# Fused linear attention and GELU MLP: w_in tiles 8 and 9 of chunk 0 side by side, k of batch 0 from a second queue, batch 1's kv and x by halves

## The chip, the cores and the metric

One core of a Trainium2 chip. The metric is the device time of one execution in microseconds (us); each kernel is timed several times, the median is quoted, and the runs of the other kernel are taken in the same rounds on the same chip. A profile's times count from its first instruction ("the span", about 1.8 us shorter than the device time here).

## The reference, cut to what matters

```python
# q, k, v: (8 batches, 8 heads, 576, 64) f32
q_s = softmax(q, over head_dim);  k_s = softmax(k, over seq)
kv  = einsum("bhsd,bhse->bhde", k_s, v)
x   = einsum("bhsd,bhde->bhse", q_s, kv)      # -> (4608 tokens, 512)
h   = x @ w_in                                # 512 x 2048
out = gelu(h) @ w_out                         # exact gelu (erf); 2048 x 512
```

## The kernel before

Nine chunks of 512 tokens: one per batch, and one of the batches' rests. A chunk's w_in stage (64 matmuls of 128x512, a gelu per tile of 4) is followed by its w_out stage (64 matmuls). Attention of a later batch is woven into these. The argument is about chunk 0, where the loads still arrive, and the passage to chunk 1:

```python
touch = singles.tile([16, 4, 2], FP32)        # tiny first reads of k, v, w_in, w_out, from ScalarE
for i, a in enumerate((k[0]..., v[0]..., moe_w_in[...], moe_w_out[...])):
    nc.scalar.dma_start(out=touch[:, i, :], in_=a)
load_main(0, "q", q, 2)                       # two halves, from SyncE
load_pair(0, "k", k, 2)
load_pair(0, "v", v, 4)
wi = [load_wi(i) for i in range(5)]
...
h_phase(0, {...casts of w_in and w_out...}, groups={0: 2, 4: 4}, ybanks=(6, 8))
...
for t in range(12): y_part(t, range(J))       # chunk 0's w_out stage, 4 matmuls a step
tp_step(1, 0); tp_step(1, 1)                  # transposes of batch 1's q
y_part(12, range(J)); y_part(13, range(J))
kv_step(1)                                    # 72 small matmuls, then VectorE's norm
y_part(14, range(J)); y_part(15, (0, 1))
y_out(0, yps[0], 0); y_out(0, yps[1], 1)      # VectorE
x_mm(1, 0); x_mm(1, 1)                        # batch 1's x, then its copies
y_part(15, (2, 3))
h_phase(1, ...)                               # chunk 1's w_in stage
```

`groups={0: 2, 4: 4}` says which tiles of w_in's stage run side by side (step by step over the contraction); `ybanks` says which tiles use a bank of the idle w_out pool in PSUM, the memory that matmuls write to.

The softmax here doesn't subtract the row's maximum and nothing guards it: scores larger than these inputs give would overflow.

## Time and profile before

| | before |
|---|---|
| time, median (first three runs) | 280.57 us (280.5 to 281.31) |
| TensorE busy in the profile | 98% of 278.9 us |
| q's second half of batch 0 landed | 5.78 us |
| v's last piece of batch 0 landed | 12.38 us |
| chunk 0, first w_in matmul | 14.57 us |
| chunk 0, first w_out matmul | 29.16 us |
| chunk 1, first w_in matmul | 45.44 us |
| chunk 2, first w_in matmul | 75.39 us |

The starts up to chunk 1 are those of TensorE's timeline, chunk 2's is that of its piece in the chain that ended last; their differences are taken as the length of each stage. From chunk 2 on all kernels here run alike, so the start of chunk 2 tells a kernel's lead or lag. The profile's lines are shown in the prediction.

### The profile page before, as it was taken

What the parts mean: (1) busy time and instruction counts of PE and PEld (TensorE: products, weight loads), DVE (VectorE), ACT (ScalarE), POOL (GpSimd) and SP (SyncE); (2) the same over time, 40 slices, a digit from 0 to 9 for tenths busy, and PEclk for the clock granted to TensorE, in tenths of its full rate; (3) what the DMA queues carried; (4) which work ended last, traced back from release to release, by engine and by line L of the source; (5) the groups of instructions that cost most, each with busy time, mean ns of one, the idle gap of its engine ahead of it and who ended that gap; (6) DMA issues with size and microseconds to landing.
All of it is one profiled execution on the core that took longest, in us unless ns stands there. A gap on an engine that the chain in (4) does not pass through costs nothing.

```text
span 278.9 us, 4564 instructions
## 1 busy us (share of the span) xinstructions
PE 272.2 (98%) x1922; PEld 125.8 (45%) x1922; DVE 102.1 (37%) x152; ACT 157.0 (56%) x243; POOL 33.0 (12%) x25
## 2 busy tenths in 40 slices
PE   7899999999999999999999999999999999999995
PEld 3343454444444444444444444444444444444443
DVE  3767486309753530093007500651015200130012
ACT  5747665689377816691569346943683263036400
POOL 1530050002020130004000500050005000000000
PEclk9999999999999999999999999999999999999999
DMA  7999999962993139812981189117501500120033
GB/s 237 385 405 428 399 401 407 399 257 74 305 352 64 41 109 240 329 38 73 256 349 41 40 219 384 49 66 185 119 0 75 150 2 0 75 78 0 0 78 76
DMA packets 44996, 50.10 MB, mean 180 GB/s; under 512 B 20400, under 2 KB 29872, under 8 KB 44720
## 3 DMA queue, kind: packets, MB, share of 16 engines
q1 hardware_dynamic: 44688, 49.68, 53.3%
q8 instruction: 15, 0.25, 0.3%
q10 hardware_dynamic: 288, 0.13, 0.2%
q14 instruction: 5, 0.04, 0.1%
HBM read 36.70 MB, written 9.44 MB: 165 GB/s over the span
## 4 chain that ended last, share of the span: by engine, by line
PE 91%; DMA 7%; DVE 1%; ACTq 0%; issue 0%
PE ps L308 44%; PE ps L298 42%; DMA w<-in_moe_w_in_dram 3%; DMA f<-in_v_dram 2%; PE kv L166 2%; DMA touch<-in_moe_w_in_dram 2%; PE ps L254 1%; PE ps L330 1%; DVE wi_bf L381 0%; ACTq L433 0%; PE ps L259 0%; PE ps L215 0%; PE tp L215 0%; DVE y_sb L335 0%; PE xx L254 0%
## 5 line engine op out<-in xcount | busy, mean ns | idle before, releaser
L298 PE MATMUL ps<-xT,wi_bf 128*128 128x512 bf16 x576 | 126.4, 379 | 0.3
L308 PE MATMUL ps<-wo_bf,g 128*128 128x512 bf16 x560 | 124.2, 379 | 0.0
L303 ACT ACTIVATE g<-ps 128x512 bf16<-128x512 f32 x144 | 85.2, 597 | 69.3 <-PE ps L298 69.3
L298 PEld LDWEIGHTS <-wi_bf 128*128 128x128 bf16 x576 | 56.2, 98 | 68.9 <-DVE wi_bf L381 1.0
L308 PEld LDWEIGHTS <-g 128*128 128x128 bf16 x560 | 53.9, 98 | 64.6 <-issue 0.8
L315 DVE COPY y_sb<-ps 128x512 f32<-128x512 f32 x35 | 23.9, 686 | 81.4 <-PE ps L308 81.1
L198 POOL TENSOR_TENSOR e<-e,recq 128x2048 bf16<-128x2048 bf16 (+1 forms) x9 | 25.7, 2856 | 178.1 <-DVE recq L197 150.0
L145 DVE CAST v_aug<-f 128x576 bf16<-128x576 f32 x26 | 17.9, 745 | 46.9 <-DMA f<-in_v_dram 46.9
L196 DVE TENSOR_REDUCE qsum<-e 128x16 f32<-128x1024 bf16 (+1 forms) x13 | 21.0, 1615 | 13.9 <-ACT e L133 13.9
L280 ACT CAST xT<-ps 128x512 bf16<-128x512 f32 x19 | 10.3, 589 | 26.7 <-PE ps L254 17.1
L133 ACT ACTIVATE e<-f 128x512 bf16<-128x512 f32 (+1 forms) x42 | 20.5, 556 | 2.4 <-DMA f<-in_q_dram 2.0
L138 ACT ACTIVATE ek<-f 128x2304 bf16<-128x2304 f32 (+1 forms) x10 | 17.2, 1730 | 1.8 <-DMA f<-in_k_dram 1.8
L278 DVE CAST xT<-ps 128x512 bf16<-128x512 f32 x15 | 9.7, 687 | 17.5 <-PE ps L254 14.6
L79 ACT ACT_TABLE_LOAD x9 | 11.5, 1283 | 2.8 <-issue 2.6
L415 PE MATMUL ps<-zeros 128*128 128x512 f32 (+1 forms) x14 | 8.6, 764 | 1.5 <-DVE zeros L447 1.5
L133 ACT ACT_TABLE_LOAD x7 | 9.0, 1283 | 0.1
L381 DVE CAST wi_bf<-w 128x512 bf16<-128x512 f32 x12 | 7.4, 661 | 2.6 <-DMA w<-in_moe_w_in_dram 2.3
L166 PEld LDWEIGHTS <-ek 64*64 64x64 bf16 x576 | 6.3, 105 | 2.6 <-issue 1.1
L166 PE MATMUL kv<-v_aug,ek 64*64 64x65 bf16 x576 | 6.9, 193 | 0.0
L198 DVE TENSOR_TENSOR e<-e,recq 128x1024 bf16<-128x1024 bf16 x4 | 6.4, 1606 | 0.1
L254 PE MATMUL ps<-qT,kvc 64*64 64x512 bf16 x60 | 5.0, 390 | 1.0 <-DVE kvc L177 1.0
L408 DVE CAST wo_bf<-w 128x2048 bf16<-128x2048 f32 (+1 forms) x4 | 4.4, 1090 | 3.9 <-DMA w<-in_moe_w_out_dram 3.9
(35 smaller groups left out, 42.8 us busy)
## 6 DMA issues: line engine op xcount, KB each, us to landing
out_dram<-y_sb SPq DMA_DIRECT2D x32, 256.0 KB, 2.3
f<-in_k_dram SPq DMA_DIRECT2D x6, 1152.0 KB, 10.0
f<-in_v_dram SPq DMA_DIRECT2D x6, 1152.0 KB, 11.7
f<-in_q_dram SPq DMA_DIRECT2D x6, 1024.0 KB, 7.1
w<-in_moe_w_in_dram SPq DMA_DIRECT2D x6, 512.0 KB, 8.9
f<-in_k_dram SPq DMA_DIRECT2D x4, 576.0 KB, 10.0
f<-in_v_dram SPq DMA_DIRECT2D x8, 288.0 KB, 7.8
f<-in_q_dram SPq DMA_DIRECT2D x4, 512.0 KB, 8.5
```

The costliest lines, as they stand in the source:

```text
L79: nc.scalar.activation(out=scr[:, 1:2], in_=scr[:, 0:1], func=func)
L133: nc.scalar.activation(out=dst[:, i], in_=src[:, u], func=AF.Exp)
L138: nc.scalar.activation(out=ek[b % 2][:, i:i + n], in_=st[b]["kf"][:, i:i + n].rearrange("p x (n d) -> p x n d", n=NS), func=AF.Exp,)
L145: eng.tensor_copy(out=v_aug[b % 2][:, hp, :, 0:D], in_=st[b]["vf"][:, hp, :].rearrange("p (n d) -> p n d", n=NS),)
L166: nc.tensor.matmul(ps[c, i, half, 0:D + 1], ek[b % 2][pr, hp, n, :], v_aug[b % 2][pr, hp, n, 0:D + 1], start=(n == 0), stop=(n == NS - 1),)
L196: nc.vector.reduce_sum(out=qsum, in_=eq[:, :, hs, :], axis=AX.X)
L198: eng.tensor_tensor(out=eq[:, :, hs, :], in0=eq[:, :, hs, :], in1=recq.unsqueeze(3).to_broadcast([128, J, w, D]), op=ALU.mult,)
L280: nc.scalar.copy(out=st[b]["xT"][:, hp, :], in_=ps)
L298: nc.tensor.matmul(ps, wi_bf[:, dm, t * 128:(t + 1) * 128], xT[:, dm, :], start=(dm == 0), stop=(dm == NDM - 1),)
L303: nc.scalar.activation(out=g[:, t, :], in_=ps, func=AF.Gelu)
L308: nc.tensor.matmul(ps, st[c]["g"][:, t, j * 128:(j + 1) * 128], wo_bf[:, t, :], start=(t == 0), stop=(t == NDF - 1),)
L315: nc.vector.tensor_copy(out=y_sb, in_=ps)
```

## The change

Its intent: read k first and with real data instead of a touch; let each cast of w_in feed two matmuls; load batch 1's last v pair between the last two rows of w_out; cut batch 1's kv and x in halves so that TensorE can work on w_out while these arrive.

```diff
# load_pair: the first piece of k of batch 0 from ScalarE's queue
+            h0 = i * n
+            if b == 0 and name == "k" and i == 0:
+                nc.scalar.dma_start(out=f[:, 0, :], in_=src[:, 0, :])
+                h0 = 1
+            nc.sync.dma_start(out=f[:, h0:(i + 1) * n, :], in_=src[:, h0:(i + 1) * n, :])
# q and k are now issued ahead of the touches; the touch of k is gone (cut)
-    load_pair(1, "v", v, 4)
-    load_wo_end(wo[3])
+    for hp in range(3):
+        load_v1(hp)
+    load_wo_row(wo[3], 2)
+    load_v1(3)
+    load_wo_row(wo[3], 3)
-    }, groups={0: 2, 4: 4}, ybanks=(6, 8))
+    }, groups={0: 2, 4: 4, 8: 2}, ybanks=(6, 8))
-    for hp in range(3):
+    for hp in range(HP):
         cast_v(1, hp, nc.gpsimd)
# the passage into chunk 1 (cut: the x_tile and xx lines, cast_v(1, 3), the place of the last cast_wo)
-    kv_step(1)
+    kv_mm(1, 0)
+    kv_norm(1, 0, 1)
     y_part(14, range(J))
-    y_part(15, (0, 1)) ... y_out of 0 and 1 (cut)
+    x_mm(1, 0)
+    kv_mm(1, 1)
+    x_evac(1, 0, "s"); x_evac(1, 1, "s")
+    kv_norm(1, 1, 2)
+    y_part(15, range(J))
+    y_out(0, yps[0], 0)
+    y_out(0, yps[1], 1, "s")
     x_mm(1, 1)
     x_evac(1, 2)
-    x_evac(1, 3)
-    y_part(15, (2, 3))
+    x_evac(1, 3, "s")
```

More of the change, by code (lines that the diff above doesn't have):

```diff
@@ L97, in load_pair, with load_v1 @@
         for i in range(parts):
-            nc.sync.dma_start(out=f[:, i * n:(i + 1) * n, :], in_=src[:, i * n:(i + 1) * n, :])
+            h0 = i * n
[3 more added lines that the diff above has]
+            nc.sync.dma_start(out=f[:, h0:(i + 1) * n, :], in_=src[:, h0:(i + 1) * n, :])
+    def load_v1(i):
+        if i == 0:
+            st[1]["vf"] = f32in.tile([128, HP, NS * D], FP32, tag="vf", name="f")
+        src = v[1].rearrange("h (p n) d -> (h p) (n d)", n=NS)
+        nc.sync.dma_start(out=st[1]["vf"][:, i, :], in_=src[i * 128:(i + 1) * 128, :])
     def load(b):
@@ L311, in y_mm, with y_out @@
         )
-    def y_out(c, ps, j):
+    def y_out(c, ps, j, eng="v"):
         y_sb = moe_sb.tile([128, DM], FP32, tag="y_sb")
-        nc.vector.tensor_copy(out=y_sb, in_=ps)
+        if eng == "v":
+            nc.vector.tensor_copy(out=y_sb, in_=ps)
+        else:
+            nc.scalar.copy(out=y_sb, in_=ps)
         if c < B:
@@ L398, in load_wo, with load_wo_row @@
         return w
-    def load_wo_end(w):
+    def load_wo_row(w, c):
         src = moe_w_out[3 * 512:4 * 512, :].rearrange("(p c) f -> p c f", c=4)
-        for c in (2, 3):
-            nc.sync.dma_start(out=w[:, c], in_=src[:, c])
+        nc.sync.dma_start(out=w[:, c], in_=src[:, c])
     def cast_wo(i, w, c0=0, n=4, eng="v"):
@@ L425, in warm_x @@
                 )
-    touch = singles.tile([16, 4, 2], FP32)
-    for i, a in enumerate((k[0].rearrange("h (p n) d -> (h p) (n d)", n=NS)[0:128:8, 0:2],
-                           v[0].rearrange("h (p n) d -> (h p) (n d)", n=NS)[0:128:8, 0:2],
+    load_main(0, "q", q, 2)
+    load_pair(0, "k", k, 2)
+    touch = singles.tile([16, 3, 2], FP32)
+    for i, a in enumerate((v[0].rearrange("h (p n) d -> (h p) (n d)", n=NS)[0:128:8, 0:2],
                            moe_w_in[0:128:8, 0:2], moe_w_out[0:512:32, 0:2])):
         nc.scalar.dma_start(out=touch[:, i, :], in_=a)
-    load_main(0, "q", q, 2)
-    load_pair(0, "k", k, 2)
     load_pair(0, "v", v, 4)
@@ L511 @@
     tp_step(1, 1)
-    cast_v(1, 3)
     load(3)
     cast_wo(3, wo[3], 2, 1, "s")
+    cast_wo(3, wo[3], 3, 1, "s")
     y_part(12, range(J))
     y_part(13, range(J))
-    kv_step(1)
-    cast_wo(3, wo[3], 3, 1, "s")
+    kv_mm(1, 0)
+    kv_norm(1, 0, 1)
     y_part(14, range(J))
-    y_part(15, (0, 1))
-    y_out(0, yps[0], 0)
-    y_out(0, yps[1], 1)
     x_tile(1, 0, psum_a, "a")
     x_tile(1, 1, psum_h, "h")
+    x_mm(1, 0)
+    kv_mm(1, 1)
+    x_evac(1, 0, "s")
+    x_evac(1, 1, "s")
+    kv_norm(1, 1, 2)
+    y_part(15, range(J))
+    y_out(0, yps[0], 0)
+    y_out(0, yps[1], 1, "s")
     xx = psum_a.tile([128, 2, M], FP32, tag="a2", name="xx")
     st[1]["x2"], st[1]["x3"] = xx[:, 0], xx[:, 1]
-    x_mm(1, 0)
     x_mm(1, 1)
-    x_evac(1, 0, "s")
-    x_evac(1, 1, "s")
     x_evac(1, 2)
-    x_evac(1, 3)
-    y_part(15, (2, 3))
+    x_evac(1, 3, "s")
     y_out(0, yps[2], 2)
```

## The prediction

> **What bounds the kernel now.** I read the page first (busy shares, slices), then the chain that ended last, then who waited for whom on TensorE in the first 30 us, then single instructions of chunk 0, because the first two views say that only the front can move. The page's busy line and the clock line of its slices:
>
> ```profile
> PE 272.2 (98%) x1922; PEld 125.8 (45%) x1922; DVE 102.1 (37%) x152; ACT 157.0 (56%) x243; POOL 33.0 (12%) x25
> ...
> PEclk9999999999999999999999999999999999999999
> ```
>
> TensorE is busy 98% of 278.9 us at full clock; no other engine passes 56%. The chain that ended last, in order of time (start, us, what):
>
> ```profile
> 5.97 6.41 DMA f<-in_v_dram
> 12.38 0.02 issue
> 12.40 9.27 DMA w<-in_moe_w_in_dram
> 21.67 0.02 issue
> 21.69 1.16 DVE wi_bf L381 x2
> 22.85 0.05 issue
> 22.89 6.43 PE ps L298 x29
> 29.33 10.36 PE ps L308 x48
> ...
> 45.51 13.96 PE ps L298 x64
> ...
> 75.39 13.81 PE ps L298 x64
> ```
>
> The reader is to see two regimes. Up to 22.9 us loads set the end: batch 0's v, then w_in, then two VectorE casts of w_in. From there on the chain is TensorE alone, without a hole to the last output. A full chunk's 64 matmuls of w_in take 13.81 us, 0.2158 us each, and nothing in this change touches that. So all there is to win is (a) the time before chunk 0's first w_in matmul, (b) holes inside chunk 0's w_in stage and (c) holes between chunk 0's w_out stage and chunk 1.
>
> (b) TensorE's timeline has these lines (start, us, ..., count, idle before):
>
> ```profile
> 14.23 0.41 PE L254 MATMUL ps<-qT,kvc 64*64 64x512 bf16 x4 [0.60 <-DVE kvc L177]
> 14.57 14.75 PE L298 MATMUL ps<-xT,wi_bf 128*128 128x512 bf16 x64
> 29.16 10.52 PE L308 MATMUL ps<-wo_bf,g 128*128 128x512 bf16 x48
> ```
>
> From 14.57 to 29.16 are 14.59 us for 64 matmuls that need 13.81: 0.78 us of holes. The waits of the weight loads between 14 and 29 us name most of them (total, times, longest):
>
> ```profile
> PEld L298 <- DVE wi_bf L381: 1.0, 2, 0.6
> ```
>
> The single matmul starts place them: 18.47 to 18.89 (0.20 us over the pitch, released by a gelu that frees a PSUM tile), 21.91 to 22.37 (0.25 over) and 22.37 to 22.90 (0.31 over). The last two, 0.56 us, are tile 8's third and fourth contraction steps waiting for the casts of w_in's fourth block: its first half landed at 20.43, its second at 21.67, and each cast takes 0.62 us.
>
> (c) From 29.33 to 45.51 the chain has 16.18 us; 64 w_out matmuls (13.81), 16 transposes (0.90), 72 kv (0.71) and 8 x (0.56) make 15.98. Holes and mode changes are worth 0.2 us.
>
> **What the Trainium skill says.** "TensorE: Matmul & The Clock Gate", section "Back-to-back issue gap", has N/2.4 + 2.5 ns for a single-matmul gap, 216 ns at N=512; the trace's 215.8 ns agrees, though the page also gives 131 ns as the sustained value, which this trace contradicts. "DMA: Bandwidth & Descriptors", section "Issuing engines are not separate DMA queues": transfers of Scalar and Sync run on the same 16 DMA engines and interleave. The trace agrees in that DMA is near full (0.9 or more) in the slices from 7 to 56 us while nearly all is issued by one engine; a second issuer finds no spare bandwidth. "PSUM — Partial Sum Buffer", section "PSUM bank collisions raise a hardware error": two engines may not access one bank at once, reads included. The kernel before has both copies of the two-bank tile xx on VectorE, so its trace cannot show it; in the new order ScalarE's copy of the second half does wait for VectorE's of the first.
>
> **The change, part by part.**
>
> *1. k of batch 0 first, part of it from ScalarE, its touch gone.* Same bytes, one 0.3 MB piece of k (128 x 2304 B = 0.295 MB) now queued at 0.74 us beside q instead of a tiny touch. q's halves (0.524 MB) landed at 4.41 and 5.78, so the rate is 0.383 MB/us and the piece costs 0.77 us. Whichever way the two queues interleave, q's second half lands after it: later by 0.45 (if the cold ramp before 3 us overlaps) to 0.77. That half feeds exp, row sum, normalisation (VectorE, ends 10.35), transposes at 10.49, first kv half at 11.46. From there by durations, without the waits for v: first kv norm 11.99, x 12.54, second kv half 12.78, its norm, x 13.82, first w_in matmul 14.17, against a measured 14.57 that v's last piece (landed 12.38, GpSimd cast to 13.11) sets. So the q path has 0.40 us of slack, and the start slips by 0.05 to 0.37 us. The v path may come up to 0.3 us earlier, since k's first reads (5 to 6 us, 300 GB/s against 383) now overlap q; that gains nothing as long as q decides.
>
> *2. Tiles 8 and 9 side by side.* No instruction added. Each cast step now feeds two matmuls (0.43 us) against 0.62 us of a cast, with a head start: counting from 21.69, step three is due at 22.55 (cast done near 22.31) and step four at 22.98 (cast done 22.85). The 0.56 us of holes close. Tile 9 needs a PSUM tile that gelu 4 frees at 21.83; it is due at 21.91, so at most a hole of some 0.02 us. With a slipped start there is even more room. w_in stage ends at 28.58 + slip against 29.16: gain 0.56 - slip, 0.2 to 0.5.
>
> *3. v's last pair between rows 2 and 3, cast on GpSimd.* Before, v's pieces landed at 39.20, 39.89, 40.61, 41.36, the rows at 41.99 and 42.62. Swapped, row 2 lands near 41.3 and pair 3 near 42.0; GpSimd casts (0.67 us) to 42.7. The second kv half is due near 43.8 less the gain, so it is hidden. Row 2 is cast (0.62, ScalarE) by 41.9, due at 42.6 less the gain; row 3 by 43.25, due at 44.2 less the gain. All hold for gains up to 0.6; the old order would have waited for row 2 (cast by 42.64, due at 42.95 less the gain) for gains over 0.3. So this part protects part 2 rather than gains.
>
> *4. kv and x by halves, copies moved.* Same matmuls, two more switches between 128-row and 64-row work, about 0.1 us each by the starts around 44.3 (44.04 to 44.35 is 0.31 against a 0.22 pitch). It removes the 0.06 hole and some waits in sequence, and PE alone reaches chunk 1 at 45.49 against 45.44. New ends: y_out of tile 0 follows the second kv norm on VectorE (44.33 to 44.85, then 0.69) and frees chunk 1's first PSUM tile at 45.5, some 0.05 late; x's last copy on ScalarE follows VectorE's (46.3 + 0.6 = 46.95) where the fourth step is due at 46.83, 0.15 late with the wait's latency. Net cost of 4: about 0.2 us.
>
> Sum: 0.35 (part 2 less slip, middle) - 0.2 = 0.15 us, and with the chance that q is delayed less, 0.25. From 280.57: about **280.3 us**.
>
> **The rivals.** First, the stream gets faster, q is barely later: the k dip disappears, start 0.2 earlier, gain 0.8, 279.8. For it: 5 to 6 us runs below rate although the queues are full. Against: q's bytes now share from the first packet. Second, the touches come too late: they queue behind the k piece, and first reads of v and w_in run cold; v's later pieces wait for touch landings before being issued. Touches landed at 4.6 to 7.5 before, some 1.4 apart; shifted by 1.5 us they still precede v's data (8.5 on) but barely w_in's issue. That would cost up to 0.8 us, 281.1. Third, chunk 1's head stalls more than counted: ScalarE runs two x copies, y_out, another x copy before the first gelu; each missed step is 0.2 to 0.6 us, 280.7 to 281.
>
> **Range and chances.** The holes are 0.78 + 0.2 us, so a gain over 1 us needs an earlier start, which v's landing limits to a few tenths; a loss over 0.7 needs two rivals at once. The three times before spread 0.8 us around 280.57. Range 279.6 to 280.9. Two per cent is 5.6 us, beyond all of these: same 0.98.
>
> **What the changed profile would show.** Part 1: q's second half lands at 6.2 to 6.6 and the first w_in matmul starts at 14.6 to 14.95; wrong if it starts before 14.5. Part 2: the wait for VectorE's w_in casts gone from the weight loads, stage length 14.0 to 14.1 us instead of 14.59. Part 3: no wait for rows 2, 3 or GpSimd's last cast. Part 4: waits of chunk 1's first matmuls on ScalarE or VectorE, 0.2 us in all. From chunk 1's second tile to the end everything is shifted alike. A slower first chunk of w_in loads, or a new hole above 0.3 us, would make it wrong.

## The result, and the profile after

280.93 us (280.8 to 281.83, 6 runs) against 280.53 (280.42 to 281.31, 6 runs). The ratio is 1.0012, 95% interval 0.9994 to 1.0029: the same within 2%, and unclear in sign. Ratios are the mean time of one kernel's fast runs over that of the other's of the same rounds, so not quite the ratio of the medians.

TensorE's timeline of the changed kernel answers to the three lines shown of before (start, us, engine, line, what, count, idle before). A few matmul records are missing from this trace (x62, x47), so starts are read, not counts:

```profile
14.58 0.41 PE L266 MATMUL ps<-qT,kvc 64*64 64x512 bf16 x4 [0.62 <-DVE kvc L189]
14.92 14.19 PE L310 MATMUL ps<-xT,wi_bf 128*128 128x512 bf16 x62
28.94 10.52 PE L320 MATMUL ps<-wo_bf,g 128*128 128x512 bf16 x47
...
45.38 0.60 PE L310 MATMUL ps<-xT,wi_bf 128*128 128x512 bf16 x2
```

The start is 0.35 us later (14.92 against 14.57), the w_in stage 0.57 shorter (14.02 against 14.59), the passage to chunk 1 0.16 longer (16.44 against 16.28). Chunk 2 starts at 75.47, so chunk 1 itself took 30.09 us against 29.95, 0.14 longer. The four differences sum to +0.08 us, which is the distance of the two profiles' chunk 2 starts.

The weight loads' waits between 14 and 29 us no longer name VectorE's w_in casts (total, times, longest):

```profile
PEld L266 <- DVE kvc L189: 0.7, 1, 0.7
PEld L310 <- issue: 0.5, 2, 0.3
```

And the front of the chain that ended last now goes through q where it went through v and w_in (start, us, what):

```profile
1.26 5.44 DMA f<-in_q_dram
6.70 0.02 issue
6.72 0.76 ACT e L145 x2
...
8.02 1.91 POOL e L210
...
13.21 0.41 PE ps L266 x4
...
14.58 0.41 PE ps L266 x4
14.99 0.32 PE ps L310
```

q's second half lands at 6.70 us instead of 5.78. The loads behind it come earlier than before, not later: v's last piece at 11.76 (12.38 before) and w_in's fourth block at 19.83 and 21.07 (20.43 and 21.67).

The chain names q's second half, but it infers its step from ScalarE's exp of that half (ended 7.97) to GpSimd's normalisation (8.02). e8 speaks against that step: there GpSimd begins at 7.93, before the exp of the second half ends at 8.36. GpSimd normalises q's first half, VectorE the second. These are the two in before, then in the changed kernel (start, us, engine, line, what, idle before):

```profile
7.36 1.90 POOL L198 TENSOR_TENSOR e<-e,recq 128x1024 bf16<-128x1024 bf16 x1 [6.06 <-DVE recq L197]
8.62 1.72 DVE L198 TENSOR_TENSOR e<-e,recq 128x1024 bf16<-128x1024 bf16 x1
...
8.02 1.90 POOL L210 TENSOR_TENSOR e<-e,recq 128x1024 bf16<-128x1024 bf16 x1 [6.71 <-ACT e L145]
9.54 1.46 DVE L210 TENSOR_TENSOR e<-e,recq 128x1024 bf16<-128x1024 bf16 x1
```

In both, GpSimd begins 0.15 us after VectorE's reciprocals for the first half (ended 7.21 and 7.87), as in all fourteen traces, and VectorE's line ends 1.08 us after GpSimd's. That 1.08 us stands in twelve of the fourteen traces, wherever q's second half landed between 5.78 and 6.70; the exceptions are e5 and e8, where it landed after 7. So what moved the start here is q's first half: it landed 0.65 us later (5.06 against 4.41), GpSimd ended 0.65 later (9.92 against 9.27), and kv began 0.66 later (12.12 against 11.46). Before's start followed v instead, so not all of that shows in it.

### The profile page after: what moved, and what is told of

It is laid out like the page before. It is cut to its first block, busy times and chain, and to the rows that moved or that the text cites. A ratio compares the mean times of both kernels' runs of the same rounds, so it can differ in the third digit from the quotient of the medians.

```text
span 279.0 us, 4537 instructions
## 1 busy us (share of the span) xinstructions
PE 269.0 (96%) x1894; PEld 125.7 (45%) x1922; DVE 99.8 (36%) x151; ACT 158.0 (57%) x245; POOL 33.9 (12%) x26
## 4 chain that ended last, share of the span: by engine, by line
PE 93%; DMA 2%; ACT 1%; issue 1%; POOL 1%; DVE 0%; SPq 0%
PE ps L310 45%; PE ps L320 43%; DMA f<-in_q_dram 2%; PE kv L178 2%; PE ps L266 2%; PE ps L345 1%; POOL e L210 1%; ACT L79 0%; ACT e L145 0%; PE ps L227 0%; ACT qT L238 0%; PE ps L271 0%; SPq L90 0%; PE tp L227 0%; PE xx L266 0%
## 5 line engine op out<-in xcount | busy, mean ns | idle before, releaser
L320 PE MATMUL ps<-wo_bf,g 128*128 128x512 bf16 x543 | 122.1, 379 | 1.6 <-issue 1.1
L328 DVE COPY y_sb<-ps 128x512 f32<-128x512 f32 x34 | 23.2, 684 | 79.8 <-PE ps L320 76.8
L157 DVE CAST v_aug<-f 128x576 bf16<-128x576 f32 x25 | 17.1, 745 | 48.2 <-DMA f<-in_v_dram 48.2
L429 PE MATMUL ps<-zeros 128*128 128x512 f32 (+1 forms) x14 | 8.0, 716 | 1.5 <-DVE zeros L463 1.5
```

The lines of the kernel that those rows point to most:

```text
L157: eng.tensor_copy(out=v_aug[b % 2][:, hp, :, 0:D], in_=st[b]["vf"][:, hp, :].rearrange("p (n d) -> p n d", n=NS),)
L320: nc.tensor.matmul(ps, st[c]["g"][:, t, j * 128:(j + 1) * 128], wo_bf[:, t, :], start=(t == 0), stop=(t == NDF - 1),)
L328: nc.vector.tensor_copy(out=y_sb, in_=ps)
```

## The experiments

Four kernels ran on each of three chips, one series per chip; before's median was 280.66, 280.28 and 280.57 us in them, so kernels of different series are compared by their traces, or each by its ratio to before. An interval that just misses 1 (e2, e7, e12) is weak evidence, as one of several like it.

| run | what | time, us | ratio to before (95%) | start | first w_out | chunk 1 | chunk 2 |
|---|---|---|---|---|---|---|---|
| before | | 280.53 | | 14.57 | 29.16 | 45.44 | 75.39 |
| changed | | 280.93 | 1.0012 (0.9994 to 1.0029) | 14.92 | 28.94 | 45.38 | 75.47 |
| e1 | changed, again | 280.75 | 1.0005 (0.9989 to 1.0022) | 14.90 | 28.93 | 45.37 | 75.46 |
| e2 | part 1 alone | 280.40 | 0.9986 (0.9973 to 0.9998) | 14.95 | 28.97 | 45.24 | 75.20 |
| e3 | part 2 alone | 280.43 | 0.9995 (0.9974 to 1.0017) | (clock halved in this trace) | | | |
| e4 | all but part 1 | 280.58 | 0.9991 (0.9976 to 1.0005) | 14.84 | 28.86 | 45.30 | 75.39 |
| e5 | all but part 4 | 280.65 | 1.0012 (0.9999 to 1.0024) | 15.15 | 29.17 | 45.58 | 75.53 |
| e6 | changed, own bank for x's fourth tile | 280.61 | 1.0013 (0.9999 to 1.0027) | 14.88 | 28.90 | 45.34 | 75.25 |
| e7 | changed, k piece third | 280.69 | 1.0014 (1.0001 to 1.0028) | 14.93 | 29.23 | 45.67 | 75.76 |
| e8 | two k pieces ahead of q | 280.96, one run | | 15.07 | 29.10 | 45.54 | 75.63 |
| e9 | before | 281.53, one run | | 14.61 | 30.05 | 46.32 | 76.28 |
| e10 | parts 3 and 4 alone | 280.73 | 1.0011 (0.9998 to 1.0025) | 14.79 | 29.39 | 45.84 | 75.92 |
| e11 | parts 1 and 2, tile 7 in a spare bank | 280.26 | 1.0003 (0.9985 to 1.0022) | 14.94 | 28.76 | 45.04 | 75.00 |
| e12 | e11 with one warming matmul less | 280.03 | 0.9982 (0.9970 to 0.9994) | 14.71 | 28.53 | 44.80 | 74.76 |

**e1, the changed kernel again.** No edit.

> The changed kernel itself, once more, in the same rounds as its parts. Theory (from the two traces): its start is 0.35 us later, its w_in stage of chunk 0 0.57 us shorter, its passage into chunk 1 some 0.3 us longer, so the sum is about +0.08 us, ratio 1.000 to 1.0005. Rival: the +0.4 us of the first medians is real and comes from somewhere the profile does not show; then ratio 1.001 to 1.002 again.

280.75 us, and every stage as in the first trace to 0.02 us. The sum of +0.08 us is what the trace can account for; the first series' +0.4 did not come back on this chip (+0.09 by the medians), and both intervals contain 1. Of the twelve runs of the changed kernel in the two series, ten lie between 280.70 and 281.03; before's seventeen lie between 280.42 and 281.57.

**e2, part 1 alone.** The kernel before with only the first hunk of the diff and the order of q, k and touches.

> The kernel before with part 1 alone (batch 0's k piece first from ScalarE, touch of k gone). Theory: q's second half lands near 6.7, first w_in matmul at 14.9 as in the changed kernel; w_in's fourth block lands 0.6 us earlier, so with the later start its casts are ready in time and the 0.56 us of holes close without tiles 8 and 9 side by side; stage of chunk 0 14.0 us, old passage into chunk 1, so about 0.2 us faster than before (280.3). Rival: side by side is what closed the holes; then the stage stays 14.3 to 14.6 us and the time is 0.1 to 0.35 us above before.

As the theory had it: start 14.95, stage 14.02 us without any pairing of tiles 8 and 9, passage 16.27. TensorE's timeline of e2:

```profile
14.95 14.18 PE L303 MATMUL ps<-xT,wi_bf 128*128 128x512 bf16 x62
28.97 10.52 PE L313 MATMUL ps<-wo_bf,g 128*128 128x512 bf16 x47
...
45.24 1.51 PE L303 MATMUL ps<-xT,wi_bf 128*128 128x512 bf16 x6
```

So in the changed kernel parts 1 and 2 close the same holes, and only one of them is paid. Part 1 alone is faster than before by 0.14%, with an interval that just excludes 1; in the traces its chunk 2 starts 0.19 us earlier.

**e3, part 2 alone.** Before with `groups={0: 2, 4: 4, 8: 2}`.

> The kernel before with part 2 alone (tiles 8 and 9 side by side). Theory: start 14.57, stage 14.02 us, the 0.56 us of casts' holes gone; then the old order of loads makes the second kv half and row 2 of w_out wait 0.3 us in all, net about 0.25 us faster (280.3). Rival: side by side does not close them (tile 9's PSUM tile or the casts still late): stage 14.3 us or more and no gain.

280.43 us in the median, five of the six runs between 280.23 and 280.55; the interval is wide because of the first, 282.07, which is the one that was profiled. Its windows tell why (stretch, length, busy of PE, PEld, DVE, ACT, POOL with counts, PEclk, DMA share, GB/s):

```profile
9.30:15.00 5.70, 4.20 (x104) 2.25 (x104) 3.26 (x7) 4.62 (x6) 2.82 (x5) 0.97 1.05 390
15.00:18.20 3.20, 2.98 (x11) 1.14 (x9) 2.76 (x5) 0.58 (x1) 1.60 (x3) 0.51 1.05 402
18.20:30.60 12.40, 12.31 (x57) 5.49 (x57) 7.63 (x12) 8.40 (x15) 0.00 (x0) 1.00 1.03 415
```

From 14.70 to 18.12 us the granted clock was a half, and the matmuls came every 0.427 us instead of 0.216. This trace can't test part 2; e4 and e10 do in part, and e7 better. The same mean clock, 0.994, marks two of the changed kernel's twelve runs (281.83 and 281.81) and two of e11's six; none of before's 32 runs with a listed clock has it (0.998 at the lowest). These runs count in the ratios. I did not test what brings it on.

**e4, all but part 1.** The changed kernel with before's touches and k loads.

> The changed kernel without part 1 (touches and k as before). Theory: the later q was what delayed the start; start back at 14.57, stage 14.02, new passage into chunk 1 0.3 us longer than the old, so about 0.25 us faster than before and 0.3 faster than the changed kernel. Rival: the start slips for another reason or the stage waits again for casts because w_in lands 0.6 us later than in the changed kernel; then as slow as the changed kernel or slower.

The interval contains 1; the trace is half as expected. The w_in stage is 14.02 us, so no hole is left at tile 8 without part 1 either; how much of that is due to part 2 is seen under e10 and e7. But the start is 14.84, not 14.57: in this run v's second piece landed at 11.22 (10.90 before) and its last at 12.65, and kv's first half stops for 0.34 us until GpSimd has cast the second piece. The start follows v here and q in the changed kernel.

**e10, parts 3 and 4 alone.** e4 without `8: 2`. It stands here because it is e4's counterpart.

> The kernel before with parts 3 and 4 alone (swapped loads, kv and x by halves, copies moved). Theory: start and w_in stage as before (holes of up to 0.56 us at the casts), passage from the first w_out matmul to chunk 1's first w_in matmul 16.44 us instead of 16.28 and a hole of 0.18 us at its seventh step, so 0.2 to 0.3 us slower than before. Rival: the passage costs only in the changed kernel, where it comes earlier; then within 0.1 of before.

Start 14.79 as e4's 14.84, w_in landed 0.4 us later than in e4 (20.65 and 21.89 against 20.24 and 21.48), stage 14.60 us against e4's 14.02. The waits of weight loads in e4 (total, times, longest):

```profile
PEld L261 <- DVE kvc L184: 0.7, 1, 0.7
PEld L305 <- issue: 0.3, 1, 0.3
PEld L305 <- POOL wi_bf L388: 0.2, 1, 0.2
```

And e10's, where the casts stand first:

```profile
PEld L305 <- DVE wi_bf L391: 1.0, 2, 0.6
PEld L261 <- DVE kvc L184: 0.7, 1, 0.7
```

The holes at tile 8 are 0.26 and 0.31 us (start to start 0.48 and 0.52 against 0.216); e4 has none. But this pair can't credit pairing with all of it: w_in's fourth block landed 7.10 us after the start in e10 and 6.64 in e4, and by the ends of e4's casts an unpaired tile 8 would have waited an estimated 0.12 us there. e7, below, tells more. Passage 16.45 us and chunk 1 30.08 us: parts 3 and 4 cost their 0.3 us here too, at another time of arrival, so the rival falls.

**e5, all but part 4.** The changed kernel with before's order from `kv_step(1)` to chunk 1.

> The changed kernel with part 4 undone: batch 1's kv in one piece, x after it, the old copies; parts 1 to 3 stay. Theory: the new passage into chunk 1 is what costs, 0.17 us of TensorE mode changes and 0.12 us more of a wait in chunk 1's first tiles; undone, chunk 1 starts near 45.2 as with part 1 alone, time 280.4, some 0.3 below the changed kernel. Rival: the swapped loads (part 3) cost as well, GpSimd's cast of the last pair or row 3 late; then a wait for GpSimd or for row 3 shows and the time stays at 280.6 to 280.8.

280.65 us, not the 280.4 that I had expected: the start of the profiled run is 15.15, since q's second half landed at 7.17. The passage is 16.41 us, of which 0.13 is new: kv's 72 matmuls take 0.84 us (42.25 to 43.09) against 0.71, since its second half waits for GpSimd's cast of the last v pair, which landed at 41.91. Chunk 1 takes 29.95 us, as in before. So the hole at chunk 1's head (0.14 us) belongs to part 4, the passage is 16.28 without the kv wait, and part 3 under the old order is a small cost of its own. On the time the run is inconclusive.

**e6, a bank of its own for x's fourth tile.**

```diff
-    st[1]["x2"], st[1]["x3"] = xx[:, 0], xx[:, 1]
+    st[1]["x2"] = xx[:, 0]
+    x_tile(1, 3, psum_a, "a")
```

> The changed kernel, with x's fourth tile in a PSUM bank of its own (the one that x's first tile left) so that ScalarE's copy need not wait for VectorE's of the third. Theory: the copy starts 0.7 us earlier, near 45.5, the hole of 0.18 us at chunk 1's fourth step closes, total 0.15 to 0.2 us below the changed kernel (280.55). Rival: the step waits for something else anyway (VectorE's third copy, 46.2); then the hole stays and the time as well.

ScalarE's timeline around 45 us in the changed kernel (start, us, what, idle before):

```profile
44.81 0.60 ACT L330 COPY y_sb<-ps 128x512 f32<-128x512 f32 x1
46.23 0.59 ACT L292 CAST xT<-xx 128x512 bf16<-128x512 f32 x1 [0.82 <-DVE xT L290]
```

The same in e6:

```profile
44.76 0.60 ACT L330 COPY y_sb<-ps 128x512 f32<-128x512 f32 x1
45.48 0.59 ACT L292 CAST xT<-ps 128x512 bf16<-128x512 f32 x1
```

The copy no longer waits for VectorE's, and runs 0.75 us earlier; chunk 1 takes 29.91 us against 30.09. The prediction expected this wait from "PSUM — Partial Sum Buffer", section "PSUM bank collisions raise a hardware error". That section forbids two engines to access the same bank of a partition at once; the two halves of xx lie in two banks, so it doesn't ask for the wait. The wait came with the two halves being one tile, behind whose read by VectorE the program put ScalarE's. As a time e6 can't be set beside the changed kernel, which did not run on that chip.

**e7, the k piece third.** The same piece, issued from ScalarE behind the touches of v and w_in.

> The changed kernel with the same k piece from ScalarE issued third, behind the touches of v and w_in. Theory: it was the piece's place ahead of q that delayed the start; now q's second half lands near 5.8, v's last near 12, the first w_in matmul at 14.2 to 14.5 instead of 14.9, and the time is 0.4 to 0.7 below the changed kernel (280.1 to 280.4). Rival: the 0.6 us faster stream came from having k first, so it is lost, v lands at 12.4 and the start is 14.57 as before (280.4); or holes at the casts come back.

q's second half is back at 6.00 us and v's last piece stays early, 11.77; x's last matmuls are at 14.14, 0.44 earlier than in the changed kernel. That is what q's first half gains (GpSimd's normalisation ends at 9.48 against 9.92, kv begins at 11.68 against 12.12), not the 0.70 us of the second. The gain is lost at the next step (idle before, releaser):

```profile
14.14 0.41 PE L265 MATMUL ps<-qT,kvc 64*64 64x512 bf16 x4 [0.62 <-DVE kvc L188]
14.93 14.46 PE L309 MATMUL ps<-xT,wi_bf 128*128 128x512 bf16 x64 [0.38 <-POOL wi_bf L392]
```

w_in's first block landed at 14.18 us in this run, 13.17 in the changed kernel, and its cast is what the first w_in matmul waits for. So the piece's place ahead of q is what delays q, as the theory says, but the 0.4 us that it frees were not to be had in this trace. The five times range from 280.17 to 281.17, and the ratio's interval lies just above 1. Why w_in's first block was late is open.

This run is also the better test of part 2. w_in's fourth block landed 7.17 us after the start, as late as in before and e10 (7.10 each), and yet no weight load waits for VectorE's casts, only for GpSimd's of the first two blocks (total, times, longest):

```profile
PEld L309 <- POOL wi_bf L392: 1.3, 2, 0.7
```

The stage of 14.30 us is 14.02 and a hole of 0.27 at tile 2 (16.88 to 17.36). By the ends of the casts an unpaired tile 8 would have waited an estimated 0.37 us.

**e8, two pieces ahead of q.** The first two k pieces from ScalarE, none of them from SyncE.

> The suspected cost doubled: both 0.295 MB pieces of k's first half go from ScalarE ahead of q. Theory: each piece costs q 0.77 us, so q's second half lands near 7.4 and the first w_in matmul starts near 15.6; as v has landed by then, nothing absorbs it, and the time is 0.6 to 0.75 above the changed kernel (281.4). Rival: the queues share evenly after the first piece and q is no later; then the start stays at 14.9.

The direction holds, the size does not: q's second half lands at 7.09 us, 0.39 later and not 0.77, and the start is 15.07, not 15.6. q's first half is no later than with one piece (4.97 against 5.06), so the second piece only slows the second half. Here and in e5 (7.17, start 15.15) VectorE begins its normalisation after GpSimd has ended, so the second half sets the start, 0.15 and 0.23 us later than in the changed kernel. In e1, e2 and e6, where it landed at 6.48 to 6.66, the starts (14.88 to 14.95) lie 9.85 or 9.86 us behind the first half (5.02 to 5.10).

**e9, before.** No edit.

> The kernel before itself, for a second trace of it. Theory: the first profile of before (span 278.9) was one of its later starts; its usual run has v's last piece at about 12.1 and a start near 14.3, span 278.3 to 278.6, so the start of the changed kernel (14.9 in every trace) lies 0.5 to 0.6 us behind the usual one, not 0.35. Rival: the trace is like the first, start 14.57, and the 0.4 us of the medians must come from elsewhere.

This theory got no support. The run was a slow one of its kind, 281.53, with the start at 14.61 as in the first trace and 15.44 us for the w_in stage: w_in's third block had begun to land late (its second quarter at 17.36 us against 16.42), its fourth landed at 21.32 and 22.56, and the waits for casts grew. Four traces at full clock have before's front (before, e9, e10, e4); their starts are 14.57, 14.61, 14.79 and 14.84, and none is early. What differs more is the holes behind the start. Before's quickest run in a series has a span of 278.3 us, 0.6 below the profiled 278.9, about what its 0.56 us of holes would give if they closed; no trace shows such a run, so that stays an inference.

**e11, the useful parts, and one hole more.** Part 1 and part 2, old loads and old passage, `ybanks=(6, 7)`: tile 7 rather than tile 8 takes the spare bank and does not wait for gelu 3.

```diff
-    }, groups={0: 2, 4: 4}, ybanks=(6, 8))
+    }, groups={0: 2, 4: 4, 8: 2}, ybanks=(6, 7))
```

> Parts 1 and 2 with the old loads and the old passage into chunk 1, and tile 7 instead of tile 8 of chunk 0 in a spare PSUM bank, so that it need not wait for gelu 3. Theory: start 14.9, stage 13.82 us (no hole left), passage 16.28, about 0.2 us below part 1 alone: ratio to before 0.998. Rival: tile 8 or 9 then waits for its bank, or row 2 of w_out for its cast; then as part 1 alone, 0.9986.

The stage is 13.82 us, which is 64 times 0.2159: no hole is left. Chunk 2 starts at 75.00, 0.2 below e2 as expected. The times split: four runs from 280.12 to 280.28, and two of 281.29 and 281.49 with the clock at 0.994, so the ratio is unclear.

**e12, one warming matmul less.** e11 with `warm(1)` for the second `warm(2)`, the filler matmuls ahead of batch 0's kv.

> The same with one warming matmul instead of two ahead of batch 0's kv. Theory: with q deciding the start, kv begins when the two warming matmuls end (12.12) though its operands are there near 11.75; one fewer brings the start from 14.9 to 14.65 to 14.7, another 0.2 us. Rival: something else in the chain (GpSimd's cast, VectorE's copies) holds kv or x, start unchanged; or TensorE idles longer and its clock is halved for some us in more runs.

TensorE's timeline of e12, from the warming matmul to the first w_out matmul:

```profile
11.59 0.38 PE L420 MATMUL ps<-zeros 128*128 128x512 bf16 x1
11.90 0.48 PE L171 MATMUL kv<-v_aug,ek 64*64 64x65 bf16 x36
...
13.00 0.41 PE L259 MATMUL ps<-qT,kvc 64*64 64x512 bf16 x4 [0.40 <-DVE kvc L182]
...
14.71 13.99 PE L303 MATMUL ps<-xT,wi_bf 128*128 128x512 bf16 x62
28.53 10.52 PE L313 MATMUL ps<-wo_bf,g 128*128 128x512 bf16 x47
```

kv begins at 11.90 instead of 12.14 and the start follows, 14.71. 280.03 us, 0.18% below before of the same rounds: this version beats before by 0.5 us in the medians, and by the traces the changed kernel too (chunk 2 at 74.76 against 75.47). None of its five runs had the lower clock. It also corrects a reading of the changed kernel's trace: there the x matmuls at 13.21 seemed to wait for ScalarE's gelu table (its small activation ends at 13.17); here that activation ends at 13.16 as well and x starts at 13.00. The wait is for VectorE's kv norm, and the table's end lay beside it by chance.

## Why the prediction was right or wrong

The prediction named 280.3 us, a range of 279.6 to 280.9, and 0.98 for "the same". It is the same. The median of the first series, 280.93, lies 0.03 above the range's end, that of the second, 280.75, inside it; instead of a gain of 0.25 us there is a loss of 0.1 to 0.4 that the intervals don't tell from nothing. By its steps:

- **What bounds the kernel**: right. All that the traces show happens before chunk 2, and each part moved the stage that it was said to move.
- **Part 1, q late and the start slipped**: that q's delay slips the start was right, the path was not. The prediction led it through q's second half and VectorE's normalisation; the traces lead it through the first half and GpSimd's. The second half came 0.92 us later, where 0.45 to 0.77 was said; with the predicted slack of 0.40 that would have been a slip of 0.52. The first half's 0.66 at kv, less 0.40, plus 0.09 that kv to the start took longer than reckoned (2.80 against 2.71), is the 0.35 measured. That it lies inside the predicted 0.05 to 0.37 is luck, since the first half's delay happened to fall into the range named for the second; the sum used the middle (0.21), so that term was off by 0.14. That the stream behind q gets faster was right too (0.62 us at v's last piece, where 0.3 was said), and as said it gains nothing at the start.
- **Part 2**: pairing closes such holes (e7: none at tile 8, where an estimated 0.37 us would have stood), and the stage is 14.02 us where 14.0 to 14.1 was predicted. What the prediction did not see is that part 1 closes the same holes (e2), through the later start and w_in's earlier landing, so part 2 gains nothing on top of it. No trace shows pairing alone at before's time of landing and full clock.
- **Part 3**: no wait of TensorE on rows 2 and 3 or on GpSimd's last cast in the changed kernel, as predicted. The runs show nothing that it had to protect: with part 1 the old order had no such wait in e2, nor in e11 and e12, whose w_out stages start 0.40 and 0.63 us earlier than before's and whose passages still take 16.28 and 16.27 us.
- **Part 4**: the mechanism was right, 0.2 us was said and 0.30 measured: 0.16 in the passage, where TensorE alone was taken for 0.05, and 0.14 at chunk 1's head, where the wait of ScalarE's copy behind VectorE's was named (its reason was not the bank, see e6; and 46.3 + 0.6 is 46.90 there, not 46.95). By TensorE's starts, kv's two halves take 0.41 and 0.44 us where the whole takes 0.71, and x's halves 0.24 and 0.34 where the whole takes 0.56, 0.17 us more in all; I take that for the price of entering and leaving the small matmuls once more each.
- **The sum**: 0.57 - 0.35 - 0.30 = -0.08 us, against a predicted gain of 0.15, raised to 0.25 for a chance that q would be delayed less. That raise had no support in the working, and the traces went the other way.
- **The baseline**: the holes were read from one profile of before. Before's runs spread by more than the whole effect (280.42 to 281.57), so part of the first series' 0.4 us may lie in which of its runs were met. The slip is uncertain likewise: 14.57 is the earliest of four starts with before's front (mean 14.70). Of this, e9 settled nothing.
- **The rivals**: none came about as told. The faster stream did, but with q late; touches were not too late (each landing of v and w_in was earlier than before); chunk 1's head stalled, but within what was counted.

## What to carry to other kernels

When one unit is busy 98% of the time, list the holes in front of it one by one and ask for each change which hole it closes: two changes that close the same hole are worth one, and the second may only bring its costs. A transfer put on a second queue beside the data that the start waits for can delay that data by most of its own time (here by 0.65 of an estimated 0.77 us), even if everything behind it then arrives earlier. Where a chain names what released a step, check it in a second trace in which that releaser comes later. Where the effect is a few tenths of a microsecond and the kernel's own runs spread by one, compare stage starts in traces, and take more than one trace of each kernel before you price a hole.

## What the Trainium skill lacked or had wrong

- "TensorE: Matmul & The Clock Gate", section "Back-to-back issue gap", gives 131 ns per matmul as the sustained value at N=512 for a stream of weight loads and matmuls and calls 216 ns the single gap. Here the stream of pairs runs at 215.8 ns (64 in 13.81 us in every chunk from the third on), at full clock.
- "DMA: Bandwidth & Descriptors", section "Queues, rings and completion order", says that an engine goes round between queues packet by packet. It doesn't tell what that gives at a start: the k piece on the second queue, issued within 0.01 us of q's first half, landed at 3.88 us, and q's first half, nearly twice its size, at 5.06 instead of 4.41; the piece's own time at the measured rate is an estimated 0.77 us, so q's first half paid 0.65 of it.
- "TensorEngine Tiling (Array Packing)", section "Key Properties", lacks the cost of changing between 128-row and 64-row matmuls, and no other page that I read has it: 0.31 us from start to start instead of 0.216 (44.04 to 44.35 in before, 43.09 to 43.39 in the changed kernel), and 0.15 us for cutting 72 small matmuls in two.
- "Runtime: NRT & Kernel Launch", section "Instruction fetch mechanics", lacks what an instruction fetch does to data loads, and no other page that I read says it: in every trace one 16 KB packet of the instruction queue takes 0.88 to 0.94 us of one DMA engine near 17 us (16.86 in before), and a piece of w_in that lands after it comes late, in before 2.16 us after the one before it instead of about 0.65. That one causes the other was not tested.
